# Other byte offsets, modulo 256, for TensorE's operand tiles in a fused attention and gated-MLP kernel

## The chip, the cores and the metric

The kernel runs on one core of a Trainium2 chip. The metric is device time in microseconds (us), as the median of several executions. A profile is taken of one more execution. [...]

## The reference

Eight batches of eight heads attend from 576 positions to 32 memory slots per head, and the result goes through a gated two-matrix layer:

```python
# q, k, v: (8, 8, 576, 64); phi: (8, 8, 576, 32)
a = exp(phi - max(phi, axis=2));  a = a / (sum(a, axis=2) + 1e-9)
k_m = einsum('bhsm,bhsd->bhmd', a, k);  v_m = einsum('bhsm,bhsd->bhmd', a, v)
scores = (q @ k_m.T) / 8
attn = softmax(scores over the 32 slots)
x = (attn @ v_m), heads side by side: (8 * 576, 512)
out = (sigmoid(x @ w_gate) * (x @ w_val)) @ w_out      # w_gate, w_val: 512 x 1536; w_out: 1536 x 512
```

Everything is float32.

## The kernel before, in words

`x` is never formed. For each batch `b` and pair of column blocks `f` of the gate and value weights the kernel forms `u` = (memory values) times (weights), 256 rows (8 heads by 32 slots) by 256 columns, and then multiplies it with the attention weights `at`. Each of these operands is split into an upper part (`_hi`, a rounded copy) and a lower part (`_lo`, what the rounding left), and each product is three matmuls: upper by upper, upper by lower, lower by upper.

On TensorE a matmul has a stationary operand, which a separate instruction (LDWEIGHTS, the rows of PEld) puts into the array, and a moving operand, which streams past it. A row `acc<-wo_hi,g` names the output, the moving tile and the stationary tile, in this order. The three products that fill the trace are:

- the gate products, `gate_of`: stationary `u_hi`, `u_hi`, `u_lo`, moving `at_hi`, `at_lo`, `at_hi`, twelve matmuls at a time, on 256 columns of `at` (positions 0 to 255) or 320 (256 to 575);
- the output products of the first half of the program (up to about 285 us), `out_of`: stationary `g` (upper, upper, lower part of the gated block; both parts lie in one tile), moving `wo_hi`, `wo_lo`, `wo_hi`, each 512 columns, six matmuls at a time (a "six" below). `out_left` does the same for the last 64 positions of each batch, four blocks in a row. Its stationary operand lies in a pair of `u` tiles in three calls and in a pair of `g` tiles in the fourth, so that the same twelve matmuls stand in the program with both;
- the output products of the second half, `block_product`: a scheme of seven products of 2x2 blocks, stationary `g7_hi`, `g7_hi`, `g7_lo` (in rows `g_hi`, `g_lo`), moving the two parts of a weight block in `wo_hi`, `wo_lo` or `ring`, 256 columns.

Between them stand smaller jobs: the memory keys (`kvm,e`), scores (`q,kT`), transposes (`ident,ph`) and the `u` products (`wg,vT`).

The order of work is written out by hand: a list of words (`OPENING`) for the first part, loops with tables after that, and `issue_after` links that keep each engine in that order. SBUF tiles come from pools in the order in which they are first asked for, so that the order of these first requests, with a few small `gap` tiles between, sets the byte at which each tile begins in every partition. Where a call asks for a tile and drops the result, only its place is wanted. The tiles from `note` (`z`, `nmx`, `rz`, `mx`, `zs`) are small ones for maxima, sums and their reciprocals.

Of the kernel before, what the change touches and what calls it, by code (L numbers as in the profile page):

```python
# [9 lines left out]
F32 = mybir.dt.float32  # L10
F32R = mybir.dt.float32r
# [9 lines left out]
P = 128  # L21
B, H, S, D, M = 8, 8, 576, 64, 32
DM, DFF = 512, 1536
NG = 2
# [15 lines left out]
NE = 8  # L40
# [87 lines left out]
def attn_moe_kernel(  # L128
# [12 lines left out]
    keep = ctx.enter_context(tc.tile_pool(name="keep", bufs=1))  # L141
    dram = ctx.enter_context(tc.tile_pool(name="dram", bufs=1, space=bass.MemoryType.DRAM))
    sb = ctx.enter_context(tc.tile_pool(name="att", bufs=1))
    mb = ctx.enter_context(tc.tile_pool(name="moe", bufs=1))
# [5 lines left out]
    ob = one.enter_context(tc.tile_pool(name="one", bufs=1))  # L150
# [13 lines left out]

    def note(name):

        shape = [P, 2, S // 32] if name in ("mx", "zs") else [P, NG]
        return mb.tile(shape, F32, name=name, bufs=1)

    def small_tile():  # L170
        if "two" in pools:
# [3 lines left out]
    def g_tile():  # L175
        return ob.tile([P, 2, 2, P], F32R, name="g", bufs=LAG + 1)

    def u_tiles():
        return [mb.tile([P, 2, 2, 256], F32R, name=f"u_{p}", bufs=2) for p in ("hi", "lo")]

    for name in ("z", "nmx"):
        note(name)
    mb.tile([P, 2, 2, 256], F32R, name="u_hi", bufs=2)
    for name in ("rz", "mx", "zs"):
        note(name)
    mb.tile([P, 8], F32, name="gap1")
    u_tiles()
    mb.tile([P, DM], F32, name="wo_raw")
    ob.tile([P, 16], F32, name="gap4")
    g_tile()  # L190

    ident = keep.tile([P, P], F32, name="ident")
# [17 lines left out]
        return wgs[f // 2][:, f % 2]  # L210

    keep.tile([P, 8], F32, name="gap0")
    wos = [keep.tile([P, NE, DM], F32R, name=f"wo_{part}") for part in ("hi", "lo")]

    def wo_of(f):
        return [t[:, f, :] for t in wos]
# [66 lines left out]
    late_words, rings = [], []  # L283
# [13 lines left out]
    def load_jobs(n=None, queue="stream"):  # L297

        while jobs and (n is None or n > 0):
            f, k = jobs[0]  # L300
            if (k == 2 and f >= NE and not rings) or len(waiting) == 2:
                break
            src = wo[f] if k == 2 else wgv[f].rearrange("p k n -> p (k n)")
            words = words_tile(k)
            move_words(words.rearrange("p n t -> p (n t)"), src, queue)
            words_of[f, k] = words
            waiting.append(jobs.pop(0))
            n = n and n - 1
# [53 lines left out]
    def to_f32(f, k, done=False):  # L362


        if (f, k) not in sized:
            magnitude(f, k)
        words, dst = words_of.pop((f, k)), sized.pop((f, k))
        last_conv[0] = bits_of(dst, words)
        if f < FIRST:
            return dst  # L370
        waiting.remove((f, k))
        if not done:
            refill()
        return dst

    def refill():

        if jobs and not waiting and jobs[0][1] == 2 and jobs[0][0] >= NE and not rings:

            early.close()  # L380
            pools["conv"] = later.enter_context(tc.tile_pool(name="conv1", bufs=1))
            top = ctx.enter_context(tc.tile_pool(name="top", bufs=1, side="right"))
            top.tile([P, 8], F32, name="gap2")
            rings.append(top.tile([P, 2, 7, 256], F32R, name="ring"))
        load_jobs()

    def out_hi(f, dst):
# [39 lines left out]
    def a_max(b):  # L427

        ph = loaded[b, "phi"]
        nmx = note("nmx")  # L430
        for gs in (slice(0, 1), slice(1, 2)) if b == 0 else (slice(0, 2),):
            nc.vector.tensor_reduce(nmx[:, gs], ph[:, gs, :], axis=AX.X, op=ALU.max, negate=True)  # L432
        loaded[b, "nmx"] = nmx
# [104 lines left out]
    def blocks(b, c):  # L538

        e = loaded[b, "e"]  # L540
        if b in FLAT:
            return e[:, FLAT_CUT[c]].rearrange("p (a w m) -> p a w m", a=2, m=M)
        e = e.rearrange("p (r w m) -> p r w m", r=2, m=M)
        return e if c is None else e[:, :, CUT[c].start // 32 : CUT[c].stop // 32, :]
# [111 lines left out]
    def normalize(b, c=None):  # L656
        s_sum(b, c)
        s_over(b, c)

    def s_sum(b, c=None):  # L660
        e = blocks(b, c)
        w = e.shape[2]
        zs = note("zs")[:, :, :w]
        nc.vector.tensor_reduce(zs, e, axis=AX.X, op=ALU.add)
        nc.vector.tensor_scalar_add(zs, zs, EPS)
        nc.vector.reciprocal(zs, zs)
        loaded[b, "zs", c] = zs
# [135 lines left out]
    part = {}  # L803
# [202 lines left out]
    def late_parts(k, half):  # L1006

        work, slot = works[k], k - PAIRS
        hi, lo = ring(slot, 0), ring(slot, 1)
        pieces = ((slice(4, 7), slice(5 * 256, 8 * 256)),) if half else ((slice(0, 1), slice(0, 256)), (slice(1, 4), slice(DM, DM + 3 * 256)))  # L1010
        with behind():
            for js, xs in pieces:
                nc.scalar.copy(hi[:, js], work[:, xs].rearrange("p (j x) -> p j x", x=256))
            for js, xs in pieces:
                rest(lo[:, js], work[:, xs].rearrange("p (j x) -> p j x", x=256), hi[:, js])
        if half:
            del works[k]

    def block_keep(k):
        kept_block = new_block(k)  # L1020
        for i in range(2):
            move(kept_block[:, i], ring(k - PAIRS, i).bitcast(F32))
# [5 lines left out]
    def ring(k, i):  # L1028

        if k == 2:  # L1030
            return rings[0][:, i]
        return wos[i].rearrange("p (u f) x -> p u (f x)", u=2)[:, 1 - k, : 7 * 256].rearrange("p (j x) -> p j x", j=7)

    rows_low = []
# [5 lines left out]
    def load_block(n, k, queue="stream"):  # L1040
        for i in range(2):
            move(ring(k, i).bitcast(F32), blocks_of[n * PAIRS + k][:, i], queue)
# [302 lines left out]
    def pair(b, f):  # L1345
# [5 lines left out]
        "amax": a_max, "aexp": a_exp, "T": phi_turn, "A": phi_copy, "Z": phi_sum,  # L1351
        "K": lambda b, g: keys(b, [g]), "B": keys_copy, "t": keys_turn, "V": lambda b, w: keys_keep(b, [w]),
        "S": lambda b, c: (scores_flat if b in FLAT else scores_of)(b, c), "tp": flat_turn, "tr": scores_turn, "mx": lambda b, c=None: (flat_max if b in FLAT else s_max)(b, c), "ms": lambda b, c=None: (flat_minus if b in FLAT else s_minus)(b, c), "ex": s_exp, "nz": s_sum, "nm": s_over, "tn": turn_of_e,
        "hi": lambda b, c=None: flat_hi(b, c) if b in FLAT else turn_hi(b, c, turning[b, c]),
        "lo": lambda b, c=None: flat_lo(b, c) if b in FLAT else turn_lo(b, c, turning[b, c]),
# [8 lines left out]
    for word in OPENING.replace("\n", ";").split(";"):  # L1364
# [6 lines left out]
        name = name.rstrip("'")  # L1371
# [16 lines left out]
    def new_side(b, then):  # L1388

        work = {"keys": lambda: kept_keys(b), "max": lambda: (s_max(b), s_minus(b)), "eexp": lambda: s_exp(b)}  # L1390
        work["sum"], work["turn"], work["next"] = lambda: normalize(b), lambda: turn(b), b + 1
        work["exp"], work["zsum"], work["over"] = lambda: s_exp(b), lambda: s_sum(b), lambda: s_over(b)
        if then:
            work["amax"], work["pexp"] = lambda: a_max(then), lambda: a_exp(then)
            work["exp"] = lambda: (s_exp(b), a_exp(then))
            for g in range(NG + 1):
                work[f"T{g}"] = lambda g=g: (phi_turn(then, g), phi_copy(then, g))
        return work
# [21 lines left out]
    def blocks_step(k):  # L1420
        if k in PREP:
            do, *of = PREP[k]
            {"raw": block_raw, "sums": block_sums, "parts": block_parts, "put": block_keep}[do](*of)

    refill()
    load_phi(QUAD + 1)
    side = new_side(QUAD, QUAD + 1)
# [37 lines left out]
    later.close()  # L1465
    one.close()
    tb = pools["two"] = ctx.enter_context(tc.tile_pool(name="two", bufs=1, reuse_waits="tile"))
    tb.tile([P, 32], F32, name="gap3")
    for name, shape in (("g7_hi", [P, 7, P]), ("x1", [P, 5, P])):
        tb.tile(shape, F32R if name == "g7_hi" else F32, name=name, bufs=2)  # L1470
    low = tb.tile([P, 2, 2, 256], F32R, name="u3_hi").bitcast(F32).rearrange("p r f x -> p (r f x)")
    tb.tile([P, 32], F32, name="gap5")
    rows_of = tb.tile([P, 2, 2, 256], F32R, name="u3_lo").bitcast(F32)
    rows_low.extend(rows_of[:, i] for i in range(2))
    tb.tile([P, DM], F32, name="row", bufs=2)
# [11 lines left out]
    for i, (b, n, c, k) in enumerate(order):  # L1487
# [26 lines left out]
        f = (n * PAIRS + k) * 2  # L1514
# [10 lines left out]
        if late:  # L1525
# [3 lines left out]
            if c == 0:  # L1529
                j = LATE.index(k)  # L1530
# [76 lines left out]
```

## Time and profile before

| | |
|---|---|
| time, median of 3 | 702.32 us (701.46 to 703.95) |
| the profiled execution, its own time | 705.28 us |
| span of its trace, first to last instruction | 703.5 us |
| TensorE matmuls busy | 694.6 us, 99% of the span |
| TensorE weight loads busy | 618.7 us, 88% |
| VectorE, ScalarE, GpSimd busy | 519.8 us (74%), 402.2 us (57%), 96.9 us (14%) |
| granted TensorE clock, mean | 0.994 |

The span counts from the first to the last instruction of the trace; 1.8 us of the profiled time lie around it. A matmul's own duration is from its start to its modelled end and overlaps the next matmul, so the pace of TensorE is read from the starts: the distance from one start to the next, which the text calls the step. The timeline gives starts to 0.01 us, so steps are taken over many matmuls.

### The profile page before, as it was taken

The page shows a single profiled execution, that of the slowest core. Times are in us where ns is not written, and L with a number is a line of the kernel's source. Part 1 is how long each engine was busy: PE and PEld are TensorE (multiplying, and loading weights), DVE is VectorE, ACT ScalarE, POOL GpSimd, SP SyncE. Part 2 cuts the span into 40 slices and gives each one's busy share as a digit, 9 for nine tenths or more (in the row PEclk, how much of TensorE's full clock was granted, in tenths as well). Part 3 has the DMA queues.
Part 4 walks back from the last instruction along what each step waited for, and adds up shares of the span by engine and source line. Part 5 has one row for each costly group of instructions (what it writes and reads, how often), then busy time and mean ns, then how long its engine had stood idle before and what let it go on. Part 6 is the DMA issues. An engine that isn't in the chain of part 4 may idle for free.

```text
span 703.5 us, 15880 instructions
## 1 busy us (share of the span) xinstructions
PE 694.6 (99%) x6295; PEld 618.7 (88%) x6295; DVE 519.8 (74%) x1086; ACT 402.2 (57%) x915; POOL 96.9 (14%) x135
## 2 busy tenths in 40 slices
PE   8999999999999999999999999999999999999997
PEld 6688878889878888899898989899998989999897
DVE  1688867544487887888786789777886788976766
ACT  5799786555367436554455665564654455544542
POOL 0000000000000330223212210230103201230103
PEclk9899999999999999999999999999999999999999
DMA  9968663637788673399847585991646828382635
GB/s 358 412 230 314 244 251 125 215 158 276 253 283 280 225 265 132 73 332 297 195 99 187 144 324 197 284 333 48 237 175 153 248 79 307 62 305 61 239 112 105
DMA packets 52298, 151.49 MB, mean 215 GB/s; under 512 B 5888, under 2 KB 24320, under 8 KB 50176
## 3 DMA queue, kind: packets, MB, share of 16 engines
q1 hardware_dynamic: 33904, 89.92, 35.6%
q0 software_dynamic: 16304, 57.15, 28.3%
q10 hardware_dynamic: 2016, 3.41, 1.3%
q8 instruction: 49, 0.80, 0.5%
q14 instruction: 25, 0.20, 0.1%
HBM read 111.40 MB, written 39.06 MB: 214 GB/s over the span
## 4 chain that ended last, share of the span: by engine, by line
PE 92%; DVE 3%; DMA 2%; ACT 2%; issue 1%; ACTq 0%; DVEq 0%; POOL 0%; POOLq 0%; SPq 0%
PE pu_t L258 56%; PE acc L258 36%; DMA out_dram<-left 1%; DMA ph<-in_phiT_dram 1%; DVE u_lo L248 0%; DMA out_dram<-row 0%; ACT wg L276 0%; DVE row L1293 0%; DVE ring L248 0%; ACT g L232 0%; DVE kvm L977 0%; ACT ph L226 0%; ACT kvm L276 0%; DVE sg L843 0%; DVE nmx L432 0%
## 5 line engine op out<-in xcount | busy, mean ns | idle before, releaser
L258 PE MATMUL pu_t<-at_hi,u_hi 128*128 128x256 f32 (+1 forms) x760 | 224.0, 295 | 0.0
L258 PE MATMUL pu_t<-at_hi,u_lo 128*128 128x256 f32 (+1 forms) x760 | 222.6, 293 | 0.0
L258 PE MATMUL pu_t<-at_lo,u_hi 128*128 128x256 f32 (+1 forms) x760 | 222.1, 292 | 0.0
L258 PEld LDWEIGHTS pu_t<-at_hi,u_hi 128*128 128x128 f32 x760 | 142.7, 188 | 4.3 <-issue 1.4
L258 PEld LDWEIGHTS pu_t<-at_lo,u_hi 128*128 128x128 f32 x760 | 142.8, 188 | 1.8
L258 PEld LDWEIGHTS pu_t<-at_hi,u_lo 128*128 128x128 f32 x760 | 142.7, 188 | 0.0
L248 DVE TENSOR_TENSOR g_lo<-x,g_hi 128x128 fp32r<-128x128 f32 (+2 forms) x193 | 88.3, 463 | 14.9 <-ACT g_hi L1105 13.9
L226 ACT ACTIVATE x<-pu_t 128x320 f32<-128x320 f32 (+1 forms) x128 | 52.1, 409 | 76.0 <-PE pu_t L258 74.5
L258 PE MATMUL acc<-wo_hi,g 128*128 128x512 f32 x256 | 90.9, 399 | 0.3 <-DVE g L248 0.3
L1055 DVE TENSOR_TENSOR x<-pu_t,x 128x320 f32<-128x320 f32 (+1 forms) x128 | 57.9, 453 | 44.3 <-ACT x L226 27.4
L258 PE MATMUL acc<-wo_hi,g_hi 128*128 128x256 f32 x276 | 77.6, 281 | 0.0
L258 PE MATMUL acc<-wo_lo,g_hi 128*128 128x256 f32 x276 | 76.3, 276 | 0.0
L258 PE MATMUL acc<-wo_hi,g_lo 128*128 128x256 f32 x276 | 76.3, 276 | 0.0
L248 DVE TENSOR_TENSOR u_lo<-pu_t,u_hi 128x512 fp32r<-128x512 f32 x92 | 58.2, 681 | 14.4 <-ACT u_hi L232 14.4
L258 PEld LDWEIGHTS acc<-wo_hi,g 128*128 128x128 f32 x256 | 48.0, 188 | 16.1 <-issue 5.8
L244 POOL DMA_DIRECT2D out_dram<-row x48 | 42.3, 959 | 143.0 <-DVE row L1199 130.5
L258 PEld LDWEIGHTS acc<-wo_hi,g_hi 128*128 128x128 f32 x276 | 51.8, 188 | 10.1 <-issue 9.2
L258 PE MATMUL acc<-ring,g_hi 128*128 128x256 f32 x332 | 59.7, 280 | 0.0
L258 PEld LDWEIGHTS acc<-ring,g_hi 128*128 128x128 f32 x332 | 50.5, 188 | 9.2 <-issue 6.7
L1105 ACT CAST g_hi<-x 128x512 fp32r<-128x512 f32 x63 | 39.1, 620 | 30.6 <-DVE x L1103 30.6
L232 ACT CAST u_hi<-pu_t 128x512 fp32r<-128x512 f32 x92 | 48.9, 589 | 12.4 <-PE pu_t L258 11.4
L258 PEld LDWEIGHTS acc<-wo_lo,g_hi 128*128 128x128 f32 x276 | 51.9, 188 | 0.0
(212 smaller groups left out, 1242.9 us busy)
## 6 DMA issues: line engine op xcount, KB each, us to landing
kvm<-in_kvm_dram SPq DMA_DIRECT2D x16, 1024.0 KB, 7.5
wo_hi<-block POOLq DMA_DIRECT2D x16, 896.0 KB, 5.5
wo_lo<-block POOLq DMA_DIRECT2D x16, 896.0 KB, 7.6
ring<-block POOLq DMA_DIRECT2D x16, 896.0 KB, 6.0
q<-in_qT_dram SPq DMA_DIRECT2D x16, 512.0 KB, 4.6
out_dram<-row POOLq DMA_DIRECT2D x48, 128.0 KB, 5.9
words<-in_wgv_dram SPq DMA_DIRECT2D x5, 1023.6 KB, 6.5
part<-row SPq DMA_DIRECT2D x18, 256.0 KB, 3.9
```

The lines of the kernel that those rows point to most:

```text
L226: last_act[0] = nc.scalar.activation(*args, **kw)
L232: (nc.scalar.copy if act != swapped[0] else nc.vector.tensor_copy)(to, x)
L244: last_move[queue] = queues[queue].dma_start(dst, src, **how)
L248: return nc.vector.tensor_tensor(lo, x, hi.bitcast(F32), op=ALU.subtract)
L258: last_pe[0] = do(*args, **kw)
L1055: last_prod[0] = nc.vector.tensor_tensor(x[:, :n], val, x[:, :n], op=ALU.mult)
L1105: nc.scalar.copy(gh[:, 2:6], x[:, 1:5])
```

## The change: where the tiles lie

No instruction is added, taken away or moved. Tiles are asked for in another order and the gap tiles differ, and so tiles begin at other bytes. What matters of a place here is its remainder modulo 256:

| operand | tiles | before | after |
|---|---|---|---|
| moving, upper | `wo_hi`, `at_hi`, `ring` (upper half) | 224 | 224 |
| moving, lower | `wo_lo`, `at_lo`, `ring` (lower half) | 224 | 96 |
| stationary, gate, upper | `u_hi`, `u3_hi` | 32 | 32 |
| stationary, gate, lower | `u_lo`, `u3_lo` | 160 | 32 |
| stationary, output, first half | `g` (both parts) | 224 | 32 |
| stationary, output, second half | `g7_hi` / `g7_lo` | 32 / 160 | 32 / 32 |
| `u` products, moving / stationary | `wg` / `vT` | 192 / 224 | 192 / 96 |
| scores, moving / stationary | `q` / `kT` | 224 / 192 | 96 / 192 |
| memory keys, moving / stationary | `kvm` / `e` | 224 / 224 | 96 / 96 |

In the gate and output products every slice that a matmul takes begins a multiple of 256 bytes into its tile, so that there the table holds for every matmul; in the last three rows it gives where the tile begins. During one matmul TensorE loads the stationary operand of the next, so the pairs that are read at the same time are these (stationary loaded minus moving, modulo 256; 192 is 64 below):

| while this one runs | this is loaded | gate and second half, before | and after | `out_of`, before | and after |
|---|---|---|---|---|---|
| upper stationary, upper moving | upper | 64 | 64 | 0 | 64 |
| upper stationary, lower moving | lower | 192 | 192 | 0 | 192 |
| lower stationary, upper moving | next upper | 64 | 64 | 0 | 64 |

The `ring` tile becomes one tile with 128 bytes between its halves. The sums `zs` no longer have a tile of their own: they are written over `mx`, which the step before has used up.

```diff
-        shape = [P, 2, S // 32] if name in ("mx", "zs") else [P, NG]
-        return mb.tile(shape, F32, name=name, bufs=1)
+        shape = [P, 2, S // 32] if name == "mx" else [P, NG]
+        return (keep if name in ("z", "nmx") else mb).tile(shape, F32, name=name, bufs=1)
...
-    for name in ("z", "nmx"):
+    for name in ("rz", "mx"):
         note(name)
-    mb.tile([P, 2, 2, 256], F32R, name="u_hi", bufs=2)
-    for name in ("rz", "mx", "zs"):
-        note(name)
-    mb.tile([P, 8], F32, name="gap1")
     u_tiles()
     mb.tile([P, DM], F32, name="wo_raw")
-    ob.tile([P, 16], F32, name="gap4")
     g_tile()
...
-    wos = [keep.tile([P, NE, DM], F32R, name=f"wo_{part}") for part in ("hi", "lo")]
+    wos = [keep.tile([P, NE, DM], F32R, name="wo_hi")]
+    keep.tile([P, 2, S], F32R, name="at_hi", bufs=2)
+    for name in ("z", "nmx"):
+        note(name)
+    keep.tile([P, 16], F32, name="gap1")
+    wos.append(keep.tile([P, NE, DM], F32R, name="wo_lo"))
+    keep.tile([P, 2, S], F32R, name="at_lo", bufs=2)
...
-            rings.append(top.tile([P, 2, 7, 256], F32R, name="ring"))
+            both = top.tile([P, 2 * 1792 + 32], F32R, name="ring")
+            rings.extend(both[:, o : o + 1792].rearrange("p (j x) -> p j x", j=7) for o in (1824, 0))
...
-        zs = note("zs")[:, :, :w]
+        zs = note("mx")[:, :, :w]
...
-            return rings[0][:, i]
+            return rings[i]
...
-    tb.tile([P, 32], F32, name="gap3")
...
-    tb.tile([P, 32], F32, name="gap5")
```

The one place where a row of the order reads differently is VectorE's part of the softmax. In the first batch, before the change, the sums of the exponentials go to `zs`, and the weights `e` are multiplied by their reciprocals:

```order
L595 TENSOR_TENSOR e<-pu_t,mx 128x128
L664 TENSOR_REDUCE zs<-e 128x2x8
L665 TENSOR_SCALAR zs<-zs 128x2x8
L666 RECIPROCAL zs<-zs 128x2x8
L672 TENSOR_TENSOR e<-e,zs 128x512
```

After the change the same five instructions stand in the same place of VectorE's order, with that kernel's line numbers:

```order
L597 TENSOR_TENSOR e<-pu_t,mx 128x128
L666 TENSOR_REDUCE mx<-e 128x2x8
L667 TENSOR_SCALAR mx<-mx 128x2x8
L668 RECIPROCAL mx<-mx 128x2x8
L674 TENSOR_TENSOR e<-e,mx 128x512
```

Nothing moved. The sums stand in `mx` in place of `zs`, and VectorE has read `mx` for the last time in the row ahead.

## Rows read from the trace of the kernel before

**Rows 1.** The page: span, busy time of each engine, granted clock in 40 slices.

```profile
span 703.5 us, 15880 instructions
PE 694.6 (99%) x6295; PEld 618.7 (88%) x6295; DVE 519.8 (74%) x1086; ACT 402.2 (57%) x915; POOL 96.9 (14%) x135
PEclk9899999999999999999999999999999999999999
```

**Rows 2.** TensorE's longest wait: total us, times, longest us.

```profile
PE acc L258 <- ACT ph L226: 1.6, 1, 1.6
```

**Rows 3.** Groups by shape: line, names (moving, stationary), columns, count | busy us, mean ns.

```profile
L258 PE MATMUL pu_t<-at_hi,u_hi 128*128 128x320 f32 x380 | 117.6, 310 | 0.0
...
L258 PE MATMUL pu_t<-at_hi,u_hi 128*128 128x256 f32 x380 | 106.4, 280 | 0.0
...
L258 PE MATMUL acc<-wo_hi,g 128*128 128x512 f32 x256 | 90.9, 399 | 0.3 <-DVE g L248 0.3
L258 PE MATMUL acc<-wo_hi,g_hi 128*128 128x256 f32 x276 | 77.6, 281 | 0.0
...
L258 PE MATMUL acc<-wo_lo,g 128*128 128x512 f32 x128 | 50.4, 394 | 0.0
```

**Rows 4.** Timeline of weight loads at 197.4 us: start us, duration us, names, count.

```profile
197.40 0.19 PEld L258 LDWEIGHTS pu_t<-wo_lo,u_hi 128*128 128x128 f32 x1
```

**Rows 5.** Timeline of matmuls: a 256-column gate behind a six; start of a later six.

```profile
191.50 0.28 PE L258 MATMUL pu_t<-at_hi,u_hi 128*128 128x256 f32 x1
...
192.88 0.40 PE L258 MATMUL acc<-wo_hi,g 128*128 128x512 f32 x1
...
196.01 0.40 PE L258 MATMUL acc<-wo_hi,g 128*128 128x512 f32 x1
```

**Rows 6.** Timeline: that six's end, `out_left` with stationary `u`, the 256-column gate behind.

```profile
197.40 0.40 PE L258 MATMUL pu_t<-wo_hi,u_hi 128*128 128x512 f32 x1
...
200.18 0.28 PE L258 MATMUL pu_t<-at_hi,u_hi 128*128 128x256 f32 x1
...
201.60 0.40 PE L258 MATMUL acc<-wo_hi,g 128*128 128x512 f32 x1
```

**Rows 7.** Timeline: `out_left` with stationary `g` tiles, from its first matmul to the next gate.

```profile
272.20 0.39 PE L258 MATMUL pu_t<-wo_hi,g 128*128 128x512 f32 x1
...
274.92 0.31 PE L258 MATMUL pu_t<-at_hi,u_hi 128*128 128x320 f32 x1
```

**Rows 8.** Groups by shape: the matmuls of `out_left` alone, with either stationary tile.

```profile
L258 PE MATMUL pu_t<-wo_hi,u_lo 128*128 128x512 f32 x12 | 4.7, 396 | 0.0
L258 PE MATMUL pu_t<-wo_hi,u_hi 128*128 128x512 f32 x12 | 4.7, 394 | 0.0
L258 PE MATMUL pu_t<-wo_lo,u_hi 128*128 128x512 f32 x12 | 4.7, 392 | 0.0
...
L258 PE MATMUL pu_t<-wo_hi,g 128*128 128x512 f32 x8 | 2.6, 389 | 0.0
```

**Rows 9.** Timeline: 21 output matmuls of 256 columns in the second half.

```profile
281.90 0.39 PE L258 MATMUL acc<-ring,g_hi 128*128 128x256 f32 x2
...
284.28 0.28 PE L258 MATMUL pu_t<-at_hi,u_hi 128*128 128x256 f32 x1
```

**Rows 10.** Timeline: 24 gate matmuls of 320 columns, the first two and the end.

```profile
430.25 0.30 PE L258 MATMUL pu_t<-at_hi,u_hi 128*128 128x320 f32 x1
430.39 0.31 PE L258 MATMUL pu_t<-at_lo,u_hi 128*128 128x320 f32 x1
...
433.74 0.28 PE L258 MATMUL acc<-wo_hi,g_hi 128*128 128x256 f32 x1
```

**Rows 11.** Windows: us, TensorE busy (count), granted clock, DMA share, GB/s.

```profile
274.92:281.90 6.98, 6.98 (x49) 1.00 0.85 295
...
272.20:274.92 2.72, 2.72 (x14) 1.00 0.25 92
```

**Rows 12.** Groups by shape: the `u` products.

```profile
L258 PE MATMUL pu_t<-wg,vT 64*32 64x512 f32 x736 | 50.3, 599 | 0.0
```

## The prediction

> **What bounds the kernel now.** I read the page first. TensorE's matmuls cover 99% of the span, and the granted clock is at the upper level in all slices but the second [rows 1]. TensorE's waits come next: the longest is one of 1.6 us, and the others are shorter [rows 2]. So no other engine holds TensorE back, and the time is the sum of TensorE's steps, the distances from one matmul's start to the next. A change that alters no instruction can only alter these steps, or bring a wait where there is none.
>
> Then the groups by shape [rows 3]: 1152 gate matmuls of 320 columns (three groups of 380 and twelve single ones), as many of 256, 384 output matmuls of 512 columns in the first half (256 and 128), and 1326 of 256 columns in the second (three groups of 276 of which one is shown, and 332 and 166 with `ring`).
>
> Last the timeline, for the steps. [...]
> - 256 columns, second half: 21 matmuls from 281.90 to 284.28, a step of 113.3 ns [rows 9].
> - 320 columns: 24 from 430.25 to 433.74, a step of 145.4 ns; the single ones differ, the first is 140 ns [rows 10].
> - 512 columns, a six: 196.01 to 197.40, 1.39 us, 231.7 ns each [rows 5, 6].
> - 512 columns, twelve of `out_left` with stationary `g`: 272.20 to 274.92, 226.7 ns [rows 7]. The same twelve with stationary `u`: 197.40 to 200.18, 231.7 ns [rows 6]. The two stand apart by 5 ns in their mean durations too, (396 + 394 + 392) / 3 = 394 against 389 [rows 8].
>
> The last pair is what the trace has to say on addresses, for both run the same instructions on the same moving tiles, at the same remainder 224, and only the stationary tile differs: `g` at 224 (difference 0), `u` at 32 and 160 (differences 64, 192, 64). The next weights are loaded while a matmul runs: the load of 197.40 begins with the matmul of 197.40 [rows 4, 6]. Traffic of the DMA engines doesn't explain it: the 48 gate matmuls from 274.92 ran with the DMA engines 85% busy at 6.98 / 48 = 145.4 ns, as in rows 10, and the faster twelve had a DMA share of 25% beside it [rows 11].
>
> **The change part by part.** *Output products of the first half.* The difference goes from 0, 0, 0 to 64, 192, 64, which is that of the `u` twelve, with one thing new: the moving tile alternates between 224 and 96, and no matmul of the trace does that in these products. The nearest rows for the new price are the `u` twelve, 231.7 ns, which is what a six costs already: nothing for the 64 sixes. The twelve of rows 7, and about as many ahead of them in one row with them, run at 226.7 and would lose 5 ns each, 0.2 us with those of two shorter rows of this kind. And 18 gates of 256 columns follow a six directly: twelve took 191.50 to 192.88, 1.38 us, there, but 200.18 to 201.60, 1.42 us, behind the `u` twelve [rows 5, 6]; twelve undisturbed steps are 12 x 113.3 ns = 1.36 us. 18 x 0.04 us = 0.7 us. Together +0.9 us. From the other side: if the new places let every six run at 226.7 ns (1.36 us) and every gate behind it at 1.36, the gain is 64 x 0.03 us = 1.9 us and 18 x 0.02 = 0.4 us, -2.3 us.
>
> *Gates and second half.* While a matmul runs, the load beside it keeps its difference, 64, 192, 64. If that alone counts, the cost is nothing. What is new is again the moving operand's alternation, and here it concerns all 1152 + 1152 + 1326 matmuls. No row shows it, so I bound it. Upward: the 256-column steps fall out of the even 113.3 ns into those behind the `u` twelve, 1.42 / 12 = 118 ns: (1152 + 1326) x 4.7 ns = +11.6 us; for half of them +5.8 us. Downward: the 320-column steps come close to the first of rows 10 (140 ns), to about 142: 1152 x 3.5 ns = -4.0 us. I take zero: the one thing that the trace tells apart, the difference between load and moving tile, is kept here.
>
> *The small jobs.* The `u` products (736 matmuls of 599 ns, in groups of eight that overlap [rows 12]), scores, keys and transposes change their differences as well. Their loads are narrow (32 columns) and no row shows their step at another difference, so I take zero and bound them by a shift of the size seen above, 10 ns for each of 46 groups of sixteen, 0.5 us either way.
>
> *`zs` over `mx`.* All its readers and writers are VectorE instructions in an unchanged order; an instruction starts when VectorE gets to it, as before. Zero; the cover is VectorE's own order, and its 26% of idle time [rows 1].
>
> *Tiles of the second half that reuse memory of the first.* Their borders now fall together with those of the tiles under them, so each waits for the same tiles or fewer. TensorE waits for none of them now [rows 2]. Zero.
>
> Sum: +0.9 us against the profiled execution's 705.28 us, so 706.2 us. That execution is 3.0 us above the median of 702.32; on the median the sum gives 703.2 us.
>
> [...]
>
> **The rivals.**
> 1. *The whole stream of addresses counts, and the new places suit it.* For it: the steps depend on what ran before them (a 256-column gate needs 1.42, 1.38 or 1.36 us, depending on its forerunner), so more than the pair of one matmul and one load is at work; before, lower and upper moving tiles begin at the same remainder, after they don't. Against it: the 512-column row with the new differences is the slower one of the two. It gives -2.3 us from the first half alone (700.0 us), and -6.3 us if the 320-column steps settle at 142 ns (696.0 us).
> 2. *The even steps of 256 columns break* (the other side). For it: the second half runs at a steady 113.3 ns with both moving tiles at one remainder, and the alternation takes away exactly this; one matmul in three is displaced. Against it: its differences to the loaded weights are kept. It decides from 0.8 ns per matmul on (2478 x 0.8 ns = 2.0 us); at half of the bound it gives 702.3 + 0.9 + 5.8 = 709 us.
> 3. *Addresses don't matter*: the two twelves differ by what ran before them (rows 7 follow a long row of the same kind). Then all steps stay and the time is 702.3 us. Against it: the `u` twelve still averages 231.7 ns, though it is a row of twelve of the same kind behind six more like it [rows 5, 6].
>
> **How the numbers follow.** About 0.3% of this kernel, 2.1 us, is what a measurement can tell from no change: 700.2 to 704.4 us. The forecast (the difference within a matmul decides) has 0.36, rival 1 has 0.35, rival 2 has 0.20, rival 3 has 0.09. The forecast lies within 0.3% in most cases (0.28) above it in some (0.05: a little more at the gates), rarely below it (0.03). Rival 1 is faster in nearly all of its share (0.33), rival 2 slower, rival 3 the same. That makes 0.36 faster, 0.39 same, 0.25 slower. The predicted time is 703.2 us, its own range 702 to 705. The range over all cases is 696.0 (rival 1 in full) to 708.5 (rival 2 at nearly half its bound); a steeper loss than that is left out, some 0.1, and so is a gain over 6 us, some 0.07.
>
> **What would show it.** The forecast is right if a six takes 1.39 us, the gates of 256 columns behind a six 1.42, the second half's 256-column step stays at 113.3 ns and the 320-column step at 145.4. Rival 1 shows as sixes of 1.36 us and durations of 389 ns for `acc<-wo_lo,g` in place of 394, and its larger form as 320-column durations near 305 ns in place of 310. Rival 2 shows as 256-column durations above 280 ns in the second half. Sixes still at 1.39 with gates behind them at 1.38 would be rival 3. A new wait of TensorE in the list of waits would make the whole argument wrong.

## The result, and the profile after

The changed kernel takes 711.68 us (median, 711.15 to 713.71) against 702.32 us: a ratio of 1.0134, with an interval from 1.0112 to 1.0156. It is 9.4 us slower, above the range of the prediction (696.0 to 708.5), and on the side that had a chance of 0.25.

The page after, first its span, busy times and granted clock, as in [rows 1]:

```profile
span 711.9 us, 15882 instructions
...
PE 703.3 (99%) x6295; PEld 627.4 (88%) x6295; DVE 521.3 (73%) x1086; ACT 402.4 (57%) x915; POOL 97.0 (14%) x135
...
PEclk9999999999999999999999999999999999999999
```

TensorE's waits after (total us, times, longest us), which answer to [rows 2]:

```profile
PE acc L259 <- ACT ph L227: 2.1, 1, 2.1
PE acc L259 <- POOL ident masks.py:199: 1.4, 1, 1.4
PE pu_t L259 <- ACT e L233: 0.2, 1, 0.2
PE acc L259 <- ACT kT L233: 0.2, 1, 0.2
```

TensorE has as many matmuls as before and still no wait worth naming, but its busy time is 8.7 us longer, and the granted clock is no lower (0.996 on the mean, 0.994 before). (The two instructions more in the page are semaphore instructions, one of VectorE and one of ScalarE.) So the steps themselves have grown. The groups by shape say which ones; they answer to [rows 3]:

```profile
L259 PE MATMUL pu_t<-at_hi,u_hi 128*128 128x320 f32 x380 | 118.1, 311 | 0.0
...
L259 PE MATMUL pu_t<-at_hi,u_hi 128*128 128x256 f32 x380 | 107.4, 283 | 0.0
...
L259 PE MATMUL acc<-wo_hi,g 128*128 128x512 f32 x256 | 91.4, 401 | 0.0
L259 PE MATMUL acc<-wo_hi,g_hi 128*128 128x256 f32 x276 | 78.5, 284 | 0.0
...
L259 PE MATMUL acc<-wo_lo,g 128*128 128x512 f32 x128 | 50.1, 392 | 0.0
```

A mean duration overlaps the next matmul and shows only part of a longer step, but of these rows the two groups of 256 columns went up by 3 ns, and the others moved by 2 at most, in both directions. The timeline gives the steps. First 21 output matmuls of the second half with the 24 gates behind them, beside [rows 9, 10]; then a six and the gate behind it, and the twelve of `out_left` with stationary `g`, beside [rows 5 to 7]:

```profile
430.22 0.28 PE L259 MATMUL acc<-wo_hi,g_hi 128*128 128x256 f32 x1
...
432.69 0.31 PE L259 MATMUL pu_t<-at_hi,u_hi 128*128 128x320 f32 x1
...
436.18 0.28 PE L259 MATMUL acc<-wo_hi,g_hi 128*128 128x256 f32 x1
```

```profile
189.69 0.39 PE L259 MATMUL acc<-wo_hi,g 128*128 128x512 f32 x1
...
191.08 0.28 PE L259 MATMUL pu_t<-at_hi,u_hi 128*128 128x256 f32 x1
...
192.49 0.39 PE L259 MATMUL acc<-wo_hi,g 128*128 128x512 f32 x1
...
271.60 0.40 PE L259 MATMUL pu_t<-wo_hi,g 128*128 128x512 f32 x1
...
274.38 0.30 PE L259 MATMUL pu_t<-at_hi,u_hi 128*128 128x320 f32 x1
```

The 21 took 2.47 us, 118 ns each, where 113.3 stood. The 24 of 320 columns took 3.49 us, 145.4 ns, as before. The six took 1.39 us as before, the gate behind it 1.41 (1.38 before), the twelve 2.78 (2.72 before).

These rows stand for all. The program has 136 rows of twelve or more matmuls of 256 columns, on many slices of the tiles, whose places differ by multiples of 256 bytes. Their settled step, taken here over the six steps ahead of a row's last, was 113.2 to 113.5 ns in 119 of them before; the other 17 are gates in rows of twelve. After the change it is 117.7 ns or more in all 136.

Summed from each matmul's start to the next's over the whole trace, in us (the changes are against the profiled execution of before; labels are those of the experiments below). The last `ring` matmul has none behind it and counts up to the end of the trace, 5.1 us of its row in every kernel; "all else" holds the 1.4 us ahead of the first matmul:

| steps of | before | after | e1 | e2 | e3 | e4 | e5 | e6 |
|---|---|---|---|---|---|---|---|---|
| gates, 256 columns (1152) | 133.08 | +3.92 | +1.12 | +7.21 | +6.20 | +0.45 | +2.71 | -0.01 |
| outputs, 256, `wo` (960) | 111.36 | +3.85 | +2.02 | +6.02 | +5.84 | +0.36 | +2.33 | +0.01 |
| outputs, 256, `ring` (576) | 72.75 | +2.12 | +1.10 | +0.69 | +3.24 | +2.40 | +1.11 | +0.06 |
| gates, 320 (1152) | 168.85 | +0.16 | +1.22 | +1.19 | +1.03 | -0.02 | -0.74 | -0.03 |
| outputs, 512 (432) | 102.84 | -0.11 | +0.52 | -0.39 | -0.72 | -0.44 | -0.36 | -0.43 |
| all else | 114.61 | -1.52 | -3.17 | -4.21 | -3.87 | -2.89 | -2.54 | -3.82 |
| first five rows together | | +9.94 | +5.98 | +14.72 | +15.59 | +2.75 | +5.05 | -0.40 |
| median against median of before, same session | | +9.36 | +5.89 | +13.82 | +15.67 | +3.12 | +5.29 | -0.26 |

"All else" is lower in every kernel, since the execution of before that was profiled had a slower start (its granted clock was 0.50 for 6.8 us, in the second slice of [rows 1], and for 3.4 us in the changed kernel's; its time was 3.0 us above its median). Without it the steps of the five kinds account for each median to within 1 us. In the changed kernel 9.9 us lie in the 2688 matmuls of 256 columns, 3.7 ns for each, and next to nothing elsewhere.

### The profile page after: what moved, and what is told of

Read it like the earlier page. It is cut to its first block, busy times and chain, and to the rows that moved or that the text cites. A ratio compares the mean times of both kernels' runs of the same rounds, so it can differ in the third digit from the quotient of the medians.

```text
span 711.9 us, 15882 instructions
## 1 busy us (share of the span) xinstructions
PE 703.3 (99%) x6295; PEld 627.4 (88%) x6295; DVE 521.3 (73%) x1086; ACT 402.4 (57%) x915; POOL 97.0 (14%) x135
## 4 chain that ended last, share of the span: by engine, by line
PE 97%; DMA 1%; DVE 1%; ACT 0%; issue 0%; DVEq 0%; POOL 0%; POOLq 0%; SPq 0%
PE pu_t L259 59%; PE acc L259 38%; DMA ph<-in_phiT_dram 1%; DVE row L1295 0%; ACT ph L227 0%; DVE nmx L434 0%; DVEq L1603 0%; DVE x L1295 0%; POOL ident masks.py:199 0%; POOL ident masks.py:197 0%; POOLq masks.py:199 0%; SPq L245 0%; DVEq L1295 0%; POOLq L1597 0%
## 5 line engine op out<-in xcount | busy, mean ns | idle before, releaser
L259 PE MATMUL acc<-wo_lo,g_hi 128*128 128x256 f32 x276 | 77.9, 282 | 0.0
L259 PE MATMUL acc<-ring,g_hi 128*128 128x256 f32 x332 | 61.4, 284 | 0.0
L259 PEld LDWEIGHTS acc<-wo_hi,g_lo 128*128 128x128 f32 x276 | 52.4, 190 | 0.0
```

The costliest lines, as they stand in the source:

```text
L259: last_pe[0] = do(*args, **kw)
```

## Experiments

What had to be told apart: is it the lower moving tile that does it, the stationary tiles, their differences, the place in memory itself, or what runs around the matmuls? A placement is written below as three numbers, modulo 256 and counted from the upper moving tile: where the lower moving, the upper stationary and the lower stationary tile lie. For gates and for outputs of 256 columns, before is (0, 64, 192) and after is (128, 64, 64). The outputs of 512 columns were (0, 0, 0). Ratios of timed runs carry their 95% interval.

**e1: the changed kernel with the lower moving tiles back in line, (0, 64, 64).** Against the changed kernel:

```diff
+    mb.tile([P, 32], F32, name="gap3")
...
-    keep.tile([P, 16], F32, name="gap1")
+    keep.tile([P, 48], F32, name="gap1")
...
-            both = top.tile([P, 2 * 1792 + 32], F32R, name="ring")
-            rings.extend(both[:, o : o + 1792].rearrange("p (j x) -> p j x", j=7) for o in (1824, 0))
+            both = top.tile([P, 2 * 1792], F32R, name="ring")
+            rings.extend(both[:, o : o + 1792].rearrange("p (j x) -> p j x", j=7) for o in (1792, 0))
```

> The changed kernel with the lower moving tiles (wo_lo, at_lo, lower half of ring) put back to 224, all stationary tiles left at 32; the differences are then 64, 64, 64. Theory A, the displaced lower moving tile breaks the even steps: the 256-column step returns to 113.3 ns and the time to 701 to 704 us. Theory B, it is the stationary tiles, all at one place: the step stays near 117.8 ns and the time near 711 us.

Measured: 707.88 us, ratio 1.0083 (1.0064 to 1.0101), which is neither theory's time but lies between them. The timeline shows why. Two rows of 24 gates, with the same instructions and the same places:

```profile
288.19 0.28 PE L260 MATMUL pu_t<-at_hi,u_hi 128*128 128x256 f32 x1
...
290.91 0.28 PE L260 MATMUL acc<-ring,g_hi 128*128 128x256 f32 x1
...
306.50 0.28 PE L260 MATMUL pu_t<-at_hi,u_hi 128*128 128x256 f32 x1
...
309.33 0.28 PE L260 MATMUL pu_t<-ring,g_hi 128*128 128x256 f32 x1
```

The first took 2.72 us, 113.3 ns each, the second 2.83, 117.9 each. So one placement can run at two paces: of the 136 rows, 77 settled at 113.3 ns and 59 at 117.7 or 117.8. Putting the lower moving tiles back gives only part of the time back.

**e2: the kernel before with only the lower moving tiles of `wo` and `at` 128 bytes further, (128, 64, 192); the `ring` products keep (0, 64, 192).** That holds for the products that fill the trace: the tiles of the small jobs (`q`, `kvm`, `vT`) lie as after the change, and the sums are written over `mx`. The part that moves the lower tiles, against the kernel before:

```diff
-    wos = [keep.tile([P, NE, DM], F32R, name=f"wo_{part}") for part in ("hi", "lo")]
+    wos = [keep.tile([P, NE, DM], F32R, name="wo_hi")]
+    keep.tile([P, 2, S], F32R, name="at_hi", bufs=2)
+    for name in ("z", "nmx"):
+        note(name)
+    keep.tile([P, 16], F32, name="gap1")
+    wos.append(keep.tile([P, NE, DM], F32R, name="wo_lo"))
+    keep.tile([P, 2, S], F32R, name="at_lo", bufs=2)
```

> The stationary places of the kernel before (u and g7 at 32 and 160, g at 224), with wo_lo and at_lo alone moved to 96; both halves of ring stay at 224. Theory A: the 256-column steps of the gates and of the products with wo are near 117.8 ns, those with ring near 113.3 ns, 1980 matmuls x 4.5 ns = 9 us, so 710 to 712 us. Theory B: steps of 113.3 ns everywhere, 702 to 704 us.

Measured: 715.81 us, 1.0195 (1.0175 to 1.0216), worse than the whole change and above the 710 to 712 us of theory A. The `ring` products are a control within the run; 21 of them, and the 24 gates behind:

```profile
304.70 0.28 PE L263 MATMUL acc<-ring,g_hi 128*128 128x256 f32 x1
...
307.10 0.28 PE L263 MATMUL pu_t<-at_hi,u_hi 128*128 128x256 f32 x1
...
309.98 0.29 PE L263 MATMUL pu_t<-ring,g_hi 128*128 128x256 f32 x1
```

The control: 2.40 us, 114.3 ns. The gates: 2.88 us, 120.0 ns. Moving the lower moving tiles costs more alone than together with the stationary ones, so the parts don't add up.

**e3: every tile at one remainder, (0, 0, 0).** The moving tiles are asked for as in e2, with `gap1` at 48 columns, and the gaps about the stationary tiles differ; parts of it, against the kernel before:

```diff
+    mb.tile([P, 16], F32, name="gap3")
...
-    mb.tile([P, 8], F32, name="gap1")
...
-    ob.tile([P, 16], F32, name="gap4")
...
+    keep.tile([P, 48], F32, name="gap1")
```

> All moving and all stationary tiles at 224, all differences 0. Theory A: even steps everywhere since no moving tile is displaced, sixes at 1.36 to 1.39 us, 700 to 703 us. Theory B: the stationary tiles lie at one place, so steps near 117.8 ns and 710 us or more.

Measured: 717.66 us, 1.0244 (1.0192 to 1.0296), the slowest of all. 21 outputs with `ring`:

```profile
279.27 0.40 PE L260 MATMUL acc<-ring,g_hi 128*128 128x256 f32 x2
...
281.79 0.28 PE L260 MATMUL pu_t<-at_hi,u_hi 128*128 128x256 f32 x1
```

2.52 us, an even 120.0 ns. All 136 rows settled at 119.2 to 120.2 ns. In the products that fill the trace, this kernel and the one before differ only in the places of the loaded tiles against the moving ones, and a settled matmul of 256 columns costs 6.7 ns more. So the load's place against the moving tile cost 15.6 us here in the five kinds of the table above, and 15.7 us between the medians.

**e4: the kernel before with `wo`, `at`, `u`, `g` and `g7` 32 bytes further, differences kept; `ring` stays, so that its products become (0, 96, 224).**

```diff
-    keep.tile([P, 8], F32, name="gap0")
+    keep.tile([P, 16], F32, name="gap0")
...
-            top.tile([P, 8], F32, name="gap2")
```

> The kernel before with wo, at, u, g and g7 all 32 bytes further (moving at 0, a multiple of 64; ring stays at 224). If only differences count: steps as before for gates and wo products, and the products with ring, whose difference changes to 96 and 224, may lose their even step (498 matmuls x 4.5 ns = 2.2 us): 702 to 705 us. Theory C, a start that is no multiple of 64 bytes costs one step of 16 columns in each matmul (6.7 ns of the 113.3): 256-column steps of 107 to 109 ns where the moving tile lies at 0, up to 1980 x 4.5 ns = 9 us faster, 693 to 697 us.

Measured: 705.11 us, 1.0041 (1.0028 to 1.0055). Rows of 24 gates and of 21 outputs with `wo` settled at the 113.3 ns of before. So theory C falls: no row of 256 columns settled at 107 to 109 ns. Its 6.7 ns for 16 columns were shown by no run when it was written; in m1 below, at (0, 0, 0), the 64 columns from 256 to 320 take 26.65 ns, 6.66 for 16. Most of the 3 us (2.4) is in the `ring` products, whose differences alone changed:

```profile
278.51 0.40 PE L258 MATMUL acc<-ring,g_hi 128*128 128x256 f32 x2
...
280.99 0.28 PE L258 MATMUL pu_t<-at_hi,u_hi 128*128 128x256 f32 x1
```

2.48 us for 21, 118 ns. So shifting all tiles of a product by 32 bytes left its settled step alone, and shifting some of them against the others did not.

**m1: matmuls alone, 64 placements in steps of 64 bytes.** Rows of 36 in the kernel's pattern, with no work for the other engines beside them. Transfers to the output run during the first 32 us alone, beside the first rows:

```python
for w, d, a, b in PATTERNS:      # 256, 320, 512 columns; 4 x 4 x 4 places
    o = ps.tile([P, 512], F32, name="p")
    for r in range(REPS):
        st, mv = (s[a], s[a], s[b])[r % 3], (m[0], m[d], m[0])[r % 3]
        matmul(o[:, :w], st, mv[:, :w], start=(r == 0), stop=(r == REPS - 1))
```

> Not the reference's work: a kernel of matmuls alone, rows of 36 in the triple order (upper by upper, upper by lower, lower by upper) with nothing else on the core, for 256, 320 and 512 columns and all 64 placements of lower moving, upper and lower stationary tile at 0, 64, 128 or 192 past the upper moving tile. Theory D, the placement alone sets the steady step: it repeats the steps of the full kernels at 256 columns, 113.3 ns for (0, 64, 192), 117.8 for (128, 64, 64), 121 for (128, 64, 192), 120.0 for (0, 0, 0), something between 113 and 118 for (0, 64, 64), and the 226.7 ns of 512 columns at (0, 0, 0). Rival, what runs beside it (DMA, VectorE, ScalarE) or the bank of the result takes part: the rows come out alike, or in another order than in the kernels.

Measured (1157.25 us in all): ns from start to start, mean of the steps 13 to 35 of a row.

| placement | 256 columns | 320 | 512 |
|---|---|---|---|
| (0, 64, 192) | 113.30 | 145.61 | 231.78 |
| (128, 64, 64) | 117.96 | 145.61 | 230.96 |
| (0, 64, 64) | 117.78 | 146.70 | 233.43 |
| (128, 64, 192) | 120.35 | 146.65 | 233.35 |
| (0, 0, 0) | 120.00 | 146.65 | 226.70 |
| (0, 128, 192) | 116.52 | 144.30 | 233.26 |
| lowest of 64 | 113.30 | 144.30 | 226.70 |
| highest of 64 | 121.22 | 148.91 | 235.30 |

The paces of the kernels come back: 113.3, 118 and 120.0 at 256 columns, 145.6 at 320, 226.7 and 231 at 512. They come back with no other engine at work beside the rows and, all but the first, without DMA (from 40 to 1100 us its share is 0.00), so neither is needed for them. At 256 columns (0, 64, 192) is the only one of the 64 below 115.5, each behind the one row that happened to run ahead of it. The best placement differs for each width.

The 64 placements also test the rule of the forecast, that the difference of load to moving tile within a matmul decides. Four of them have the differences of before, 64, 192, 64: (0, 64, 192), (64, 64, 0), (128, 64, 64) and (192, 64, 128). At 256 columns they take 113.3, 118.0, 118.0 and 117.8 ns. Four have 0, 0, 0: (0, 0, 0), (64, 0, 64), (128, 0, 128) and (192, 0, 192). At 512 columns they take 226.7, 231.2, 231.4 and 233.4 ns. So equal differences don't give equal steps, at either width.

**e5: a time worked out ahead from m1.** (0, 128, 192) for gates and 256-column outputs, in the kernel before; 512 columns stay at (0, 0, 0), and the sums are written over `mx`, as in e6. Parts of the edit:

```diff
+    mb.tile([P, 2, 2, 256], F32R, name="u_hi", bufs=2)
+    note("mx")
+    mb.tile([P, 40], F32, name="gap6")
...
-    tb.tile([P, 32], F32, name="gap3")
+    tb.tile([P, 48], F32, name="gap3")
...
-    tb.tile([P, 32], F32, name="gap5")
+    tb.tile([P, 16], F32, name="gap5")
```

> The kernel before with its upper stationary tiles (u, g7) at 128 past the moving ones instead of 64, lower ones at 192 as before, g as before, sums over mx. Theory D: m1_places has 116.5 ns in place of 113.3 at 256 columns and 144.3 in place of 145.6 at 320 for this placement. 2688 matmuls of 256 columns x 3.2 ns, four fifths of it since some of these steps are disturbed before too (in the changed kernel 4.7 ns foretell 12.5 us and 9.9 were seen), is +6.9 us, 1152 x 1.3 ns is -1.5 us: +5.4 us, 706 to 709 us. Rival, only displaced lower tiles or coinciding stationary tiles cost: nothing is displaced and nothing coincides here, 702 to 703 us.

Measured: 707.41 us, 1.0069 (1.0046 to 1.0091). The matmuls of 256 columns lost 6.2 us where 6.9 was worked out, and those of 320 gained 0.7 where it was 1.5. Both signs are those of m1; that the sum, +5.3 us against +5.4, came out so closely is luck, for the two errors cancel.

**e6: the sums written over `mx`, and nothing else.** A gap of the same size stands where `zs` was, so that no place changes.

```diff
...
-        zs = note("zs")[:, :, :w]
+        zs = note("mx")[:, :, :w]
```

> The kernel before with its own places; only the sums stand in mx in place of zs, with a gap of the same size instead. All theories but one: 701 to 704 us, all steps as before. If the shared tile brought a wait it would show as VectorE or TensorE idle time, 705 us or more.

Measured: 701.86 us, 0.9997 (0.9984 to 1.0009). This part of the change costs nothing.

**m2: matmuls alone, both moving tiles in line, the stationary ones in steps of 32 bytes.** m1 with these two lines:

```diff
-STEP = 64
+STEP = 32
...
-PATTERNS = [(w, d, a, b) for w in (256, 320, 512) for d in range(4) for a in range(4) for b in range(4)]
+PATTERNS = [(w, 0, a, b) for w in (256, 320, 512) for a in range(8) for b in range(8)]
```

> Not the reference's work: the rows of matmuls of m1_places once more, with the lower moving tile in line with the upper one and the two stationary tiles at all 64 pairs of places in steps of 32 bytes. Theory D, the placement alone sets the step: the 16 pairs that m1_places had repeat their steps within 0.3 ns, (64, 192) with 113.3 ns and (0, 0) with 226.7 ns at 512 columns among them. If the place matters to 32 bytes, some pair between may be below 113.3 ns at 256 columns or 144.3 at 320; if the placement of before is at the floor of these triples, none is below 113 ns.

Measured (1158.97 us): at 256 columns (0, 64, 192) has 113.35 ns and the next best, (0, 96, 32), 115.5; at 320 the lowest is 144.30; at 512 (0, 0, 0) has 226.65. (0, 96, 224), the placement of the `ring` products in e4, has 117.8, as there. Of the 48 cases that m1 has too, 41 repeat within 0.31 ns, which was expected of all; the largest difference is 2.6 ns, at 512 columns, and at 256 columns (0, 192, 128) went from 117.7 to 115.7. So the tables of m1 and m2 give one pace of a placement, which need not be its only one. The kernel before holds the lowest in them for 256 and 512 columns.

**m3: matmuls alone, four placements behind six forerunners.** It answers what e1 left open.

```python
for n, w, (d, a, b) in ROWS:     # a forerunner, then 60 matmuls of 256 columns, 24 times
```

> This kernel does matmuls alone and not the reference's work: 24 rows of 60 matmuls of 256 columns, four placements (lower moving, upper stationary, lower stationary past the upper moving tile: 0,64,64; 0,64,192; 128,64,64; 0,128,192), each behind six different forerunners (36 of 256 columns at 128,128,0; 36 of 256 columns at 0,64,192; 24 of 320 columns at 0,64,64; six of 512 columns at 0,64,64; twelve of 512 columns at 0,64,192; twelve of 512 columns at 0,0,0). Theory D, the placement alone sets the steady step: in the second half of each row the step is 117.8 ns for 0,64,64, 113.3 for 0,64,192, 118.0 for 128,64,64 and 115 to 121 for 0,128,192, whatever ran ahead. Theory E, a row has more than one steady pace and what ran ahead picks it: 0,64,64 runs at 113.3 ns to the end of its row behind at least one forerunner, most likely the six of 512 columns at its own places, since the first-half gates of the kernel with lower moving tiles moved back ran so; and 117.8 behind others. If E also holds for the places of the change (128,64,64), some of its rows run at 113.3 too, and the loss is then one of order as well as of places.

Measured (257.32 us), ns from start to start over the second half of each row of 60:

| behind | (0, 64, 64) | (0, 64, 192) | (128, 64, 64) | (0, 128, 192) |
|---|---|---|---|---|
| 36 of 256 columns, (128, 128, 0) | 117.8 | 113.3 | 117.8 | 116.8 |
| 36 of 256, (0, 64, 192) | 113.3 | 113.3 | 117.7 | 120.0 |
| 24 of 320, (0, 64, 64) | 117.8 | 113.3 | 117.8 | 116.8 |
| 6 of 512, (0, 64, 64) | 113.3 | 113.3 | 117.9 | 116.6 |
| 12 of 512, (0, 64, 192) | 113.3 | 113.3 | 117.9 | 116.8 |
| 12 of 512, (0, 0, 0) | 117.8 | 113.3 | 117.9 | 116.8 |

Two rows of the first column, the second and the third, from the middle of each row (a timeline row stands for all equal matmuls in its window; the step is the duration less the 0.28 us of the last one, over the count less one):

```profile
29.81 4.36 PE L55 MATMUL p<-ma,sb 128*128 128x256 f32 x37
```

```profile
39.73 4.52 PE L55 MATMUL p<-ma,sb 128*128 128x256 f32 x37
```

4.08 / 36 = 113.3 ns and 4.24 / 36 = 117.8 ns, with one and the same tiles. What ran ahead picks the pace at (0, 64, 64), and it holds to the row's end. The transfers to the output, which end by 32 us here, don't pick it: of the four rows of this column behind them, two run at 113.3 and two at 117.8 ns. The places of before fell into 113.3 behind all six, after ten matmuls at the latest; those of the change behind none.

## Why the prediction was wrong

**The step that failed** is "Gates and second half: ... I take zero: the one thing that the trace tells apart, the difference between load and moving tile, is kept here." The differences of load to moving tile were kept, and the steps grew from 113.3 to 118 ns all the same: the term that I put at nothing measured 9.9 us, all of it at 256 columns. The runs put something else in its place: the pace hangs on how all three places of a row lie to each other, for each width apart, and at some placements on what ran ahead (e1, m3); the lower moving tile takes part in it as the stationary ones do. What I had to go by was one pair of rows at 512 columns, (0, 0, 0) against (0, 64, 192). The two paces were read rightly (m1 repeats them, 226.7 and 231.8 ns), but they don't show that the difference is the cause: with differences of 0, 0, 0 the other three placements of m1 take 231.2 to 233.4 ns at 512 columns too. And at 256 columns (0, 0, 0) is the slower one, by 6.7 ns (m1, e3).

**Rival 2 is what happened**, at more than the size I gave it. I priced the step rightly (118 against 113.3 ns) but took half of the matmuls and a chance of 0.20. All settled rows fell out: the full bound was 11.6 us for 2478 matmuls, and 9.9 were measured over 2688, for I had left out 210 of the last positions of the second half. It stays below 4.7 ns per matmul since the first matmuls of a row are uneven in both kernels (m3: up to ten of them): among the first ten of each row the change costs 3.2 ns per matmul, behind them 4.5. The price of a lost even pace was in the trace, in the gates behind the `u` twelve; that the even pace of before was the one to lose was the sentence "the alternation takes away exactly this", and it deserved more than the weight of a rival. The sign that I gave for it could not have told it apart: 256-column durations above 280 ns stand in [rows 3] already (281).

**The first half** came out as its terms said: the six at 1.39 us, the `g` twelve 5 ns slower per matmul (231.3 ns), the gates behind a six at 1.41 us where 1.42 was forecast. That last term was right by luck: I put it down to what stood ahead of the gates, and at (128, 64, 64) twelve gates take 12 x 118.0 ns = 1.42 us by m1 and 117.7 to 117.9 ns each behind all six forerunners of m3.

**Rival 1** fell in the size and direction that I gave it: no six at 1.36 us, `acc<-wo_lo,g` at 392 ns (394 before, 389 was its sign), 320 columns at 145.4. Its ground, that more than the pair of one matmul and one load is at work, is what m1 and m3 show. **Rival 3**, that addresses don't matter, fell with e1 to e5 and m1. **`zs` over `mx`** is nothing (e6), and **the tiles of the second half** wait for nothing new, as the list of waits shows. The small jobs stay unresolved within the 1.5 us of "all else"; their largest group, `wg,vT`, kept its 599 ns.

**What stays open.** Why (0, 64, 192) settles at 113.3 ns behind all six forerunners: the runs show that it does, and nothing in them shows the part of the chip in which loads and moving columns meet. Only four placements were tried behind six forerunners; another may have a pace of 113.3 ns too, as (0, 64, 64) has, or settle there as reliably. A kernel with separate places for the slices of 320 columns was not tried; by m1 an estimate of its gain is 1152 x 1.3 ns = 1.5 us, 0.2%, of which e5 got 0.7. None of the versions beats the kernel before by more than the noise.

## What to carry to other kernels

Where TensorE is busy all the time and its stationary tile changes at every matmul, the byte places of the moving and stationary tiles modulo 256 are worth up to 2.4% of this kernel, and moving a tile for another reason (one more small tile in a pool) can cost some of that unseen: look at the settled step over 20 matmuls before and after. Don't carry a finding from one width or one pair of tiles to another; a kernel of nothing but such rows measures them all in about a millisecond. Put different forerunners ahead of each row there, since a placement may have two paces (113.3 and 117.8 ns at (0, 64, 64) here), and choose one that falls into its good pace from all of them.

## What was not expected of the hardware

- The same row of matmuls, at the same places and the same granted clock of 1.00, has two lasting paces, 113.3 and 117.8 ns, picked by what ran ahead (m3; e1 in the kernel). At (0, 128, 192) it is 116.8 and 120.0.
- An even pace need not be a good one: (0, 0, 0) is even at 256 columns with 120.0 ns, and at 512, where it is the best of 64, with 226.65 (m2). The 256 columns more cost 106.65 ns, 0.417 ns each. An estimate from that: at 256 columns 13.3 ns of the 120.0 are not the columns' own, and 6.7 of the 113.3 at (0, 64, 192).
- The settled steps repeat within 0.4 ns without other engines' work beside them (m1), and a shift of all tiles of a product by 32 bytes leaves them as they are (113.3 ns, e4).
